# A recurrent attention with a token mixer: freely placed PSUM banks, work moved between engines, and a new order

## The chip, the cores and the metric

The kernel runs on one core of a Trainium2 chip. Its engines work side by side, each through its own list of instructions in order: TensorE (PE; its weight loads are a row of their own, PEld), VectorE (DVE), ScalarE (ACT), GpSimd (POOL), and SyncE (SP), which here only issues the transfers. TensorE writes into PSUM, a small memory of eight banks of 512 float32 columns on 128 partitions. The other memory is SBUF.

The metric is the time of the kernel on the device in microseconds, as a median over runs. "us" is microseconds.

## The reference

Two stages. The first is a linear attention with a state that decays (`B=4` batches, `H=8` heads, `S=768` tokens, `D=48`):

```python
for t in range(S):
    kt, vt, rt, wt = k[:, :, t], v[:, :, t], r[:, :, t], w[:, :, t]
    cur = einsum('bhd,bhe->bhde', u[None] * kt, vt)
    y[:, :, t] = einsum('bhd,bhde->bhe', rt, state + cur)
    state = wt[:, :, :, None] * state + einsum('bhd,bhe->bhde', kt, vt)
```

The second takes `x`, which is `y` with the heads side by side (4 x 768 x 384), and mixes the tokens of each batch:

```python
wq = x @ w_q                                   # 384 -> 64
wk = x @ w_k                                   # 384 -> 64
W_tok = 1/sqrt(64) * einsum('bsd,btd->bst', wq, wk)
mixed = einsum('bst,btd->bsd', W_tok, x)       # all tokens of the batch
out = maximum(mixed, 0.0) @ w_out              # 384 -> 384
```

All inputs and the output are float32. As no function stands between `W_tok` and `x`, the kernel computes `T = wk^T x` (64 x 384) for a batch and then `wq T`.

## The kernel before

The kernel works on 12 units, three for each batch. A unit is 256 tokens, that is two chunks of 128. Within a chunk the loop over tokens becomes matrix products. With `L` the running sum of the logarithms of `w`, `RT = r exp(L)` and `KT = k exp(-L)`, the products of tokens of one chunk are `A = KT^T RT`, masked to the past (`AM`), and the earlier chunks enter through a state `SB`. The operations of a unit, in the names that the profile uses:

| name | engine | what |
|---|---|---|
| wg, kg, rg, vg | SP queue | loads of w, k, r, v (384 KB each, v in four parts) |
| lw | ACT | logarithm of w, to bf16 |
| k, r (k16, r16), VB | POOL | casts to bf16 |
| cw | PE | running sums of lw |
| ep, en | ACT | exp(L), exp(-L), both from cw |
| kT, rT / ks | PE / DVE | transposes / copy of kT to SBUF |
| RT, qT | DVE | rT x ep, rT x ks |
| KT | DVE | ks x en, both in SBUF |
| dps, dd, Vd | PE, DVE, POOL | the term with u |
| A, AM | PE, DVE | products within a chunk, and the mask |
| kb, KD | PE, ACT | KT transposed back, scaled |
| sn, SB | PE, DVE | new state; scaled with ptm (POOL) |
| y, X | PE, ACT | output of the attention, scaled, to bf16 |
| xt, XT, qk, QK | PE, DVE, PE, ACT | X transposed; wq and wk of the unit |

After the third unit of a batch comes its mixer: T (PE), TS (ACT), mx (PE), MX (ACT, the maximum with 0), fp (PE, product with `w_out`), os (ACT), and the store.

The program's order is made by a small planner. Each step is added with an engine, an assumed duration, a rank, and the kind of buffer that it fills. The planner then plays the steps through on these assumptions: whenever an engine is free, the ready step of lowest rank for which a buffer is free starts. The instructions are emitted in the order of these starts, and each engine runs its own in that order.

```python
    NS = 2
    LATE = 60
    kinds = {"w": 3, "s": 2, "os": 3, "SB": 3}
    ...
    def wtile(dtype, name):      # two banks, three of them
        return ps.tile([C, 1024 if dtype == F32 else 2048], dtype, name=name, tag="w", bufs=3)

    def stile(dtype, name):      # one bank, two of them
        return ps.tile([C, 512 if dtype == F32 else 1024], dtype, name=name, tag="s", bufs=2)
    ...
        R = 100 * n              # n is the unit
        ...
        k16_ = add("POOL", 830, R + 10, f_c16(k16, kg), fill="k16", read=[lk_])
        r16_ = add("POOL", 830, R + 11, f_c16(r16, rg), fill="r16", read=[lr_])
        ...
        cw = add("PE", 500, R + 11, f_cw, fill="w", read=[ln])
        ...
        rT = add("PE", 460, R + 13, f_rawT("rT", r16), [kT], fill="s", read=[r16_])
        ...
        def f_KT():
            nc.vector.tensor_tensor(sb("KT", [C, 1024]), t["ks"], t["en"], ALU.mult)
        KT = add("DVE", 690, R + 14, f_KT, fill="KT", read=[ks, eno])
        ...
        for g in range(2):       # A by pairs of heads; each holds both chunks
            ...
            a = add("PE", 280, R + 20 + g, f_A, fill="w", read=[RT, KT])
            am.append(add("DVE", 1220, R + 20 + g, f_am, fill=f"AM{g}", read=[a]))
        ...
        x_ = add("ACT", 900, R + 30, f_x, read=[y0, y_])
        xt = add("PE", 360, R + 31, f_xt, [x_], fill="s")
        xts = add("DVE", 560, R + 32, f_xts, fill="XT", read=[xt])
        qk = add("PE", 680, R + 33, f_qk, [state["wts"]], fill="s", read=[xts])
        batch["qks"].append(add("ACT", 480, R + 34, f_qks, read=[qk]))
        if not last:
            return
        R += LATE
        T_ = add("PE", 1000, R + 35, f_T, batch["qks"] + batch["xs"], fill="s")
        Ts = add("ACT", 480, R + 36, f_Ts, read=[T_])
        for dt in range(NK):     # mx by thirds of the 384 channels, all tokens
            mx = add("PE", 200, R + 37 + dt, f_mx, [Ts], fill="w")
            rel.append(add("ACT", 880, R + 37 + dt, f_rl, read=[mx]))
        for ii in range(NU):     # fp by token blocks: each needs all of rel
            fp = add("PE", 1000, R + 41 + ii, f_fp, rel + [state["wts"]], fill="w")
            os_ = add("ACT", 880, R + 41 + ii, f_os, fill="os", read=[fp])
            add("SP", 1000, R + 42 + ii, f_st, read=[os_], lag=2000)
```

The bodies of most steps are cut here. In `f_T`, six matmuls (one for each chunk of the batch) sum into one bank.

Of the kernel before, what the change touches and what calls it, by code (L numbers as in the profile page):

```python
# [25 lines left out]
class Plan:  # L26
# [8 lines left out]
    def add(self, eng, dur, rank, fn, after=(), fill=None, read=(), lag=100):  # L35
        s = dict(eng=eng, dur=dur, rank=rank, fn=fn, after=[a for a in after if a is not None],
                 fill=fill, lag=lag, n=len(self.steps), out=[], reads=[])
        s["buf"] = None if fill is None else dict(kind=fill, left=0)
        for a in read:
            s["after"].append(a)  # L40
            if a["buf"] is not None:
                a["buf"]["left"] += 1
                s["reads"].append(a["buf"])
        self.steps.append(s)
        return s

    def order(self):
# [6 lines left out]
        free = dict(self.kinds)  # L54
        ready = [s for s in self.steps if not left[s["n"]]]
        running, done, eng_free, now = [], [], {}, 0
        while ready or running:
            ready.sort(key=lambda s: (s["rank"], s["n"]))
            started = True
            while started:  # L60
                started = False
                for s in ready:
                    if ready_at[s["n"]] > now or eng_free.get(s["eng"], 0) > now:
                        continue
                    if s["fill"] is not None:
                        if not free[s["fill"]]:
                            continue
                        free[s["fill"]] -= 1
# [13 lines left out]
            while running and running[0][0] <= now:  # L82
                t, n = heapq.heappop(running)
                s = self.steps[n]
                for buf in s["reads"]:
                    buf["left"] -= 1
                    if not buf["left"]:
                        free[buf["kind"]] += 1
# [10 lines left out]
def kernel(  # L99
# [48 lines left out]
    OS = [const([C, 2 * DM], F32, f"os{i}") for i in range(3)]  # L148
# [77 lines left out]
    LATE = 60  # L226
    kinds = {"w": 3, "s": 2, "os": 3, "SB": 3}
# [4 lines left out]
    for name in ("en", "ks", "qT", "RT", "KT", "ptm", "VB", "dd", "Vd", "AM0", "AM1", "KD", "XT"):  # L232
        kinds[name] = NS
    plan = Plan(kinds)

    def wtile(dtype, name):
        return ps.tile([C, 1024 if dtype == F32 else 2048], dtype, name=name, tag="w", bufs=3)

    def stile(dtype, name):
        return ps.tile([C, 512 if dtype == F32 else 1024], dtype, name=name, tag="s", bufs=2)  # L240

    def unit(n, state, batch):
# [4 lines left out]
        last = i == NU - 1  # L247
        t = {}
        R = 100 * n
        add = plan.add  # L250

        def sb(name, shape, dtype=BF16):
            t[name] = sm.tile(shape, dtype, name=name, tag=name, bufs=NS)
            return t[name]

        lw_ = add("SP", 1440, R, lambda: load(b, i, wg, w), fill="wg", lag=2000)
        lk_ = add("SP", 1440, R, lambda: load(b, i, kg, k), fill="kg", lag=2000)
        lr_ = add("SP", 1440, R, lambda: load(b, i, rg, r), fill="rg", lag=2000)

# [3 lines left out]
        lv = add("SP", 2200, R, f_lv, fill="vg", lag=2000)  # L263
# [5 lines left out]
        ln = add("ACT", 845, R + 10, f_ln, fill="lw", read=[lw_])  # L269
# [6 lines left out]
        k16_ = add("POOL", 830, R + 10, f_c16(k16, kg), fill="k16", read=[lk_])  # L276
        r16_ = add("POOL", 830, R + 11, f_c16(r16, rg), fill="r16", read=[lr_])

        def f_cw():
            t["cw"] = cw = wtile(F32, "cw")  # L280
# [7 lines left out]
        cw = add("PE", 500, R + 11, f_cw, fill="w", read=[ln])  # L288

        def f_ep():  # L290
            nc.scalar.activation(view(ep, 66, [[EW, 8], [-65, 2], [1, 64]]),  # L291
                                 t["cw"], ACT.Exp, bias=0.0, scale=1.0)
        epo = add("ACT", 1040, R + 12, f_ep, fill="ep", read=[cw])

        def f_en():
            nc.scalar.activation(sb("en", [C, 1024]), t["cw"], ACT.Exp, bias=0.0, scale=-1.0)  # L296
        eno = add("ACT", 1040, R + 12, f_en, fill="en", read=[cw])
# [9 lines left out]
        kT = add("PE", 460, R + 12, f_rawT("kT", k16), fill="s", read=[k16_])  # L307
        rT = add("PE", 460, R + 13, f_rawT("rT", r16), [kT], fill="s", read=[r16_])
# [3 lines left out]
        ks = add("DVE", 690, R + 13, f_ks, fill="ks", read=[kT])  # L312
# [3 lines left out]
        qT = add("DVE", 690, R + 13, f_qT, fill="qT", read=[rT, ks])  # L316

        def f_RT():
            nc.vector.tensor_tensor(
                view(sb("RT", [C, 1024]), 0, [[C, 8], [64, 2], [1, 64]]),  # L320
                view(t["rT"], 0, [[C, 8], [64, 2], [1, 64]]),
                view(ep, 0, [[EW, 8], [66, 2], [1, 64]]), ALU.mult)
        RT = add("DVE", 690, R + 15, f_RT, fill="RT", read=[rT, epo])

        def f_KT():
            nc.vector.tensor_tensor(sb("KT", [C, 1024]), t["ks"], t["en"], ALU.mult)  # L326
        KT = add("DVE", 690, R + 14, f_KT, fill="KT", read=[ks, eno])

        def f_ptm():
            nc.gpsimd.tensor_tensor(  # L330
                view(sb("ptm", [C, 16], F32), 0, [[2, 8], [1, 2]]),
                view(ep, 64, [[EW, 8], [0, 2]]),
                view(MB, 0, [[0, 8], [1, 2]]), ALU.mult)
        ptm = add("POOL", 220, R + 17, f_ptm, fill="ptm", read=[epo])
# [3 lines left out]
        vb = add("POOL", 830, R + 18, f_vb, fill="VB", read=[lv])  # L338
# [7 lines left out]
        dps = add("PE", 320, R + 18, f_dps, [state["ub"]], fill="s", read=[qT])  # L346
# [3 lines left out]
        dd = add("DVE", 170, R + 18, f_dd, fill="dd", read=[dps])  # L350

        def f_vd():
            nc.gpsimd.tensor_tensor(sb("Vd", [C, 2 * DM]), t["VB"],  # L353
                                    view(t["dd"], 0, [[1, 2 * H], [0, D]]), ALU.mult)
        vd = add("POOL", 1480, R + 19, f_vd, fill="Vd", read=[vb, dd])

        am = []
        for g in range(2):
            def f_A(g=g):
                t[f"A{g}"] = x = wtile(F32, f"A{g}")  # L360
                for hl in range(2):
                    for c in range(2):
                        hp = 2 * g + hl
                        col = (c * NP + hp) * C
                        for hh in range(2):
                            mm(x[:, ds(hh * 512 + (hl * 2 + c) * C, C)],
                               t["KT"][ds(hh * 64, D), ds(col, C)],
                               t["RT"][ds(hh * 64, D), ds(col, C)])
            a = add("PE", 280, R + 20 + g, f_A, fill="w", read=[RT, KT])

            def f_am(g=g):
                nc.vector.tensor_tensor(  # L372
                    view(sb(f"AM{g}", [C, 1024]), 0, [[C, 8], [1, C]]),
                    view(t[f"A{g}"], 0, [[C, 8], [1, C]]),
                    view(US, 0, [[0, 8], [1, C]]), ALU.mult)
            am.append(add("DVE", 1220, R + 20 + g, f_am, fill=f"AM{g}", read=[a]))

        nkb = 1 if last else 2

        def f_kb():  # L380
            t["kb"] = x = stile(BF16, "kb")
            for cp in range(NP * nkb):
                mm(x[:, ds(cp * C, C)], t["KT"][:, ds(cp * C, C)], ID16, trans=True)
        kb = add("PE", 240 * nkb, R + 21, f_kb, fill="s", read=[KT])

        def f_kd():
            nc.scalar.activation(sb("KD", [C, 1024])[:, ds(0, 512 * nkb)],  # L387
# [209 lines left out]
```

## Time and profile before

The kernel takes 134.17 us (median of three runs, 133.45 to 136.71). The profile is of an execution of 136.19 us, 134.5 us from the first instruction to the last.

| engine | operation | count | mean ns of one |
|---|---|---|---|
| DVE | AM, 1024 columns from PSUM | 24 | 1215 |
| DVE | KT, 1024 columns, both inputs in SBUF | 12 | 859 |
| DVE | ks, 1024 columns bf16 from PSUM | 12 | 688 |
| DVE | XT, 768 columns bf16 from PSUM | 12 | 555 |
| DVE | SB, 384 columns | 20 | 553 |
| POOL | Vd, 768 columns, both inputs in SBUF | 12 | 1478 |
| POOL | casts of k, r, v, 768 columns | 36 | 895, 872, 826 |
| ACT | ep, en, 1024 columns | 24 | 1047, 1023 |
| ACT | KD, 1024 columns (512 in four of them) | 12 | 1115 (684) |
| ACT | X, 768 columns | 12 | 900 |
| ACT | MX and os, 768 columns | 24 | 810, 805 |
| ACT | QK and TS, 384 columns | 16 | 475, 482 |
| PE | fp, 384 columns a matmul | 72 | 375 |

In such a row the shape is partitions by columns; an engine's time depends on the columns. The matmul's mean is its latency; matmuls in a row start closer together than that. A page of the profile also gives, for each engine, what ended its idle time ("A <- B" is: A stood idle until B was done), the granted clock of TensorE in tenths (PEclk, 9 is full), and the busy share of the 16 DMA engines. A timeline row gives the start, the length, the engine, the line, the operation with its output and inputs, and in brackets the idle time before it with what ended it.

### The profile page before, as it was taken

How to read it: one execution, taken by the hardware profiler on the slowest of the kernel's cores; microseconds unless marked ns; L12 is line 12 of the kernel's file. 1: busy time of each engine (PE TensorE's matmuls, PEld its weight loads, DVE VectorE, ACT ScalarE, POOL GpSimd, SP SyncE). 2: the span in 40 equal slices, each digit the busy share in tenths (PEclk: the TensorE clock that was granted, in tenths of full speed). 3: DMA queues.
4: the chain of work that ended last, by engine and by line, in shares of the span. 5: the costliest groups of instructions: out<-in, count | busy, mean ns of one | idle time of the engine just before them, and what ended most of it. 6: DMA issues, size and time to landing. Idle time of an engine off the chain costs nothing. (4 is left out here: it accounts for less than half of the span.)

```text
span 134.5 us, 3607 instructions
## 1 busy us (share of the span) xinstructions
PE 103.1 (77%) x1480; PEld 74.7 (56%) x1480; DVE 83.0 (62%) x132; ACT 80.8 (60%) x104; POOL 56.0 (42%) x79
## 2 busy tenths in 40 slices
PE   0378877787889996976898995497899976577940
PEld 0266655666656785855565784386666755432410
DVE  6457878889766588947629798219953798310000
ACT  3445565945789898358679792554789532226330
POOL 7345775647383661833852807236511404000000
PEclk9999999999999999599599999658999999975577
DMA  3999999989999999799999489699100650000084
GB/s 78 304 238 279 193 320 225 280 168 256 220 255 239 238 325 235 171 287 235 252 256 246 107 247 279 156 239 252 25 0 5 165 186 5 0 0 0 9 224 118
DMA packets 67871, 24.60 MB, mean 183 GB/s; under 512 B 64400, under 2 KB 67856, under 8 KB 67856
## 3 DMA queue, kind: packets, MB, share of 16 engines
q1 hardware_dynamic: 67440, 24.39, 73.2%
q8 instruction: 11, 0.18, 0.5%
q10 hardware_dynamic: 416, 0.00, 0.2%
q14 instruction: 4, 0.03, 0.1%
HBM read 19.66 MB, written 4.72 MB: 181 GB/s over the span
## 5 line engine op out<-in xcount | busy, mean ns | idle before, releaser
L372 DVE TENSOR_TENSOR AM<-A,US 128x1024 bf16<-128x1024 f32 x24 | 28.5, 1215 | 0.8 <-PE A L130 0.7
L353 POOL TENSOR_TENSOR Vd<-VB,dd 128x768 bf16<-128x768 bf16 x12 | 17.7, 1478 | 20.0 <-DVE dd L349 20.0
L442 ACT ACTIVATE X<-y,gx 128x768 bf16<-128x768 f32 x12 | 10.8, 900 | 10.3 <-PE y L130 10.3
L130 PE MATMUL cw<-CM,lw 64*128 64x128 bf16 x192 | 9.1, 247 | 10.0 <-ACT lw L266 10.0
L411 DVE TENSOR_TENSOR SB<-sn,ptm 128x384 bf16<-128x384 f32 x20 | 11.1, 553 | 8.7 <-PE sn L130 8.5
L130 PE MATMUL fp<-wo,MX 128*128 128x384 bf16 x72 | 15.7, 375 | 0.7 <-ACT MX L509 0.7
L266 ACT ACTIVATE lw<-wg 128x768 bf16<-128x768 f32 x12 | 10.1, 841 | 9.6 <-DMA wg<-in_w_dram 9.6
L291 ACT ACTIVATE ep<-cw 128x1024 bf16<-128x1024 f32 x12 | 12.6, 1047 | 5.5 <-PE cw L130 3.0
L337 POOL CAST VB<-vg 128x768 bf16<-128x768 f32 x12 | 9.9, 826 | 13.6 <-PE y L130 5.6
L387 ACT ACTIVATE KD<-kb,gv 128x1024 bf16<-128x1024 bf16 (+1 forms) x12 | 11.7, 971 | 5.1 <-PE kb L130 5.1
L273 POOL CAST k<-kg 128x768 bf16<-128x768 f32 x12 | 10.7, 895 | 8.7 <-DMA kg<-in_k_dram 8.6
L273 POOL CAST r<-rg 128x768 bf16<-128x768 f32 x12 | 10.5, 872 | 6.9 <-DMA rg<-in_r_dram 6.9
L311 DVE COPY ks<-kT 128x1024 bf16<-128x1024 bf16 x12 | 8.3, 688 | 8.1 <-PE kT L130 8.0
L130 PEld LDWEIGHTS <-lw 64*128 64x128 bf16 x192 | 6.7, 108 | 11.4 <-ACT lw L266 10.6
L456 DVE COPY XT<-xt 128x768 bf16<-128x768 bf16 x12 | 6.7, 555 | 10.0 <-PE xt L130 10.0
L130 PEld LDWEIGHTS <-KT 48*128 48x128 bf16 (+1 forms) x272 | 11.0, 99 | 2.5 <-DVE KT L326 0.7
L296 ACT ACTIVATE en<-cw 128x1024 bf16<-128x1024 f32 x12 | 12.3, 1023 | 0.0
L526 ACT COPY os<-fp 128x768 f32<-128x768 f32 x12 | 9.3, 805 | 4.4 <-PE fp L130 2.8
L130 PEld LDWEIGHTS <-MX 128*128 128x128 bf16 x72 | 7.5, 108 | 7.9 <-ACT MX L509 2.6
L476 ACT CAST QK<-qk 128x384 bf16<-128x384 f32 x12 | 5.7, 475 | 9.9 <-PE qk L130 9.9
L130 PEld LDWEIGHTS <-AM 128*128 128x128 bf16 x192 | 9.3, 102 | 3.5 <-DVE AM L372 1.3
L326 DVE TENSOR_TENSOR KT<-ks,en 128x1024 bf16<-128x1024 bf16 x12 | 10.3, 859 | 0.8
(61 smaller groups left out, 194.6 us busy)
## 6 DMA issues: line engine op xcount, KB each, us to landing
wg<-in_w_dram SPq DMA_DIRECT2D x12, 384.0 KB, 4.1
kg<-in_k_dram SPq DMA_DIRECT2D x12, 384.0 KB, 4.7
rg<-in_r_dram SPq DMA_DIRECT2D x12, 384.0 KB, 5.8
vg<-in_v_dram SPq DMA_DIRECT2D x48, 96.0 KB, 4.1
out_dram<-os SPq DMA_DIRECT2D x24, 192.0 KB, 3.0
wof<-in_moe_w_out_dram SPq DMA_DIRECT2D x1, 576.0 KB, 5.0
wqf<-in_moe_w_q_dram SPq DMA_DIRECT2D x1, 96.0 KB, 2.9
wkf<-in_moe_w_k_dram SPq DMA_DIRECT2D x1, 96.0 KB, 2.4
```

Of the source, the lines that this page charges most:

```text
L130: nc.tensor.matmul(o, l, rr, start=start, stop=stop, skip_group_check=True, is_transpose=trans)
L266: nc.scalar.activation(view(lw, 0, [[64, H], [512, 2], [1, D]]), view(wg, 0, [[D2, H], [D, 2], [1, D]]), ACT.Ln, bias=0.0, scale=math.exp( ...
L273: nc.gpsimd.tensor_copy(view(dst, 0, [[64, H], [512, 2], [1, D]]), view(src, 0, [[D2, H], [D, 2], [1, D]]))
L291: nc.scalar.activation(view(ep, 66, [[EW, 8], [-65, 2], [1, 64]]), t["cw"], ACT.Exp, bias=0.0, scale=1.0)
L296: nc.scalar.activation(sb("en", [C, 1024]), t["cw"], ACT.Exp, bias=0.0, scale=-1.0)
L326: nc.vector.tensor_tensor(sb("KT", [C, 1024]), t["ks"], t["en"], ALU.mult)
L337: nc.gpsimd.tensor_copy(sb("VB", [C, 2 * DM]), vg)
L353: nc.gpsimd.tensor_tensor(sb("Vd", [C, 2 * DM]), t["VB"], view(t["dd"], 0, [[1, 2 * H], [0, D]]), ALU.mult)
L372: nc.vector.tensor_tensor(view(sb(f"AM{g}", [C, 1024]), 0, [[C, 8], [1, C]]), view(t[f"A{g}"], 0, [[C, 8], [1, C]]), view(US, 0, [[0, 8], ...
L387: nc.scalar.activation(sb("KD", [C, 1024])[:, ds(0, 512 * nkb)], t["kb"][:, ds(0, 512 * nkb)], ACT.Copy, bias=0.0, scale=gv)
L411: nc.vector.tensor_tensor(view(x, 0, [[D, H], [1, D]]), view(t[f"sn{c}"], 0, [[D, H], [1, D]]), view(t["ptm"], c * 8, [[1, 8], [0, D]]), A ...
L442: nc.scalar.activation(view(X["t"], 2 * i * DM, [[DM, 2], [1, DM]]), view(t["y"], 0, [[512, 2], [1, DM]]), ACT.Copy, bias=0.0, scale=gx)
```

## The change

It has five parts.

1. PSUM becomes one tile of eight banks. The planner places each tile in any free bank, or in any two neighbouring free banks, instead of three fixed pairs and two fixed single banks. This is for tiles that waited for a slot of their kind.
2. KT, the key times its decay, goes from VectorE to GpSimd in all units but one. KD, XT, X, QK, MX and os get an engine for each unit from a table of letters. This is for evening out the engines.
3. The order comes from a table of ranks (`OFF`), one for each operation, found by a search over the planner's model. The planner also assumes other durations, and counts 260 ns after a TensorE step and 80 ns after others.
4. In the first and the last unit, en, ep, RT, KT, ptm, Vd, kb and KD are computed by chunks (512 columns at a time). In all units A and AM are now divided by chunk, and not by heads, so that y of chunk 0 needs only the first.
5. In all mixers mx is divided by token blocks and no longer by channels, so that each fp needs one MX only. In the last mixer X, XT, QK, TS, MX, fp, os and the store are halved, one half on ScalarE and the other on VectorE, and T takes its first four matmuls early.

```diff
+        banks = [True] * 8
+        def place(kind):
+            if kind == "w":
+                pairs = [x for x in range(7) if banks[x] and banks[x + 1]]
+                ...
+            ones = [x for x in range(8) if banks[x]]
+            ...
-    OS = [const([C, 2 * DM], F32, f"os{i}") for i in range(3)]
+    NOS = 4
+    OS = [const([C, 2 * DM], F32, f"os{i}") for i in range(NOS)]
...
-    LATE = 60
-    kinds = {"w": 3, "s": 2, "os": 3, "SB": 3}
+    STEP = 100
+    OFF = dict(load=-4, ln=207, c16=-50, cw=60, ex=34, rT=123, ks=-72, qT=284, RT=139, KT=27,
+               ptm=275, vb=34, dps=61, vd=-63, A=8, am=115, kb=94, kd=-148, sn=-109, sb=184,
+               y=108, x=-84, xt=129, xts=-98, qk=64, qks=249, T=148, mx=-51, rl=317, fp=103,
+               os=13, st=149)
+    ENG = dict(KT="PPPPPPPPPPDP", kd="DDADADDADDAD", xts="AAAAAAAAAAAD", x="AAADAAAAAAAA",
+               qks="DAAAAAAAAADA", rl="AAAADAAAAAAA", os="AADDDAADADAD")
+    SPLIT = (0, B * NU - 1)
+    kinds = {"os": NOS, "SB": 3}
...
+    kinds["MX"] = 4
+    PS = ps.tile([C, 4096], F32, name="PS", tag="PS")
-    def wtile(dtype, name):
-        return ps.tile([C, 1024 if dtype == F32 else 2048], dtype, name=name, tag="w", bufs=3)
+    def wtile(name):
+        return PS[:, ds(now["step"]["buf"]["bank"][0] * 512, 1024)]
...
+        end = n == B * NU - 1
+        fine = each if n in SPLIT else both
+            if lag is None:
+                lag = 260 if eng == "PE" else 80
+            step = plan.add(NAMES.get(eng, eng), dur, STEP * n + OFF[at] + more, fn, after, ...)
...
+            def f_KT(cs=cs, kte=kte):
+                e = nc.vector if kte == "D" else nc.gpsimd
+                e.tensor_tensor(sb("KT", [C, 1024])[:, cols(cs, 512)], t["ks"][:, cols(cs, 512)],
+                                t["en"][:, cols(cs, 512)], ALU.mult)
...
+        for c in range(2):
+            def f_A(c=c):          # one chunk, all heads
...
+        for p, cs in enumerate(each if end else both):
+            xe = "AD"[p] if end else ENG["x"][n]      # X; and so for XT, QK
...
+        groups = [[0, 1, 2, 3], [4], [5]] if end else [list(range(NCH))]     # T
...
         for ii in range(NU):
+            def f_mx(ii=ii):       # one token block, all channels
...
+            halves = each if end else both            # MX, fp, os, store
+                e = "AD"[p] if end else ENG["rl"][m]
```

## The prediction

> **What bounds the kernel now.** I read the page from the top, then the waits of TensorE, then three timelines (ScalarE, the SyncE queue, the end). First the busy rows and, below them, clock and DMA in 40 slices of 3.36 us.
>
> ```profile
> PE 103.1 (77%) x1480; PEld 74.7 (56%) x1480; DVE 83.0 (62%) x132; ACT 80.8 (60%) x104; POOL 56.0 (42%) x79
> ...
> PEclk9999999999999999599599999658999999975577
> DMA  3999999989999999799999489699100650000084
> ```
>
> No engine is full, the DMA engines are nearly full until slice 29 (about 97 us), then idle. So there is a load stage and, after it, 37 us in which the kernel only computes. Is the load stage bound by loads or by compute? The kernel has 12 units (256 tokens of one batch each). I take two marks per unit: the issue of its `w` load and its copy X<-y.
>
> ```profile
> 0.78 0.44 SPq L165 DMA_DIRECT2D wg<-in_w_dram  x1
> ...
> 42.35 0.58 SPq L165 DMA_DIRECT2D wg<-in_w_dram  x1
> ...
> 86.83 0.62 SPq L165 DMA_DIRECT2D wg<-in_w_dram  x1
> ```
>
> ```profile
> 17.15 0.90 ACT L442 ACTIVATE X<-y,gx 128x768 bf16<-128x768 f32 x1 [1.44 <-PE y L130]
> ...
> 72.06 0.90 ACT L442 ACTIVATE X<-y,gx 128x768 bf16<-128x768 f32 x1
> ...
> 116.04 0.90 ACT L442 ACTIVATE X<-y,gx 128x768 bf16<-128x768 f32 x1 [2.09 <-PE y L130]
> ```
>
> These are units 0, 6 and 11. From load to X unit 0 takes 16.4 us, unit 6 takes 29.7, unit 11 takes 29.2. Compute falls behind the loads, by 13 us. Its pace is (116.04 - 17.15)/11 = 8.99 us a unit. The bound is therefore the compute pipeline; loads come early and then wait for their buffers.
>
> What does a unit need of TensorE? Start-to-start distances at full clock in its timeline (20 to 45 us): cw .56, kT and rT .45 each, A .56, dps .27, kb .46, sn 2x.34, y 2x.53, xt .42, qk .65: 5.56 us. A batch adds T .97, mx 1.0, fp 18x.17 = 3.06: 5.0, or 1.68 a unit. Together 7.24 us. The pace of 8.99 is thus 1.75 us above what TensorE alone could do. Where that goes shows in TensorE's waits (total, times, longest):
>
> ```profile
> PE xt L130 <- DVE RT L319: 3.3, 4, 1.0
> ...
> PE xt L130 <- ACT KD L387: 0.8, 1, 0.8
> ...
> PE qk L130 <- DVE dd L349: 0.5, 1, 0.5
> PE dps L130 <- DVE RT L319: 0.5, 1, 0.5
> ```
>
> xt reads X, not RT. RT is the last reader of rT, and rT sits in one of the two single banks: xt waits for a bank. Such rows (these, and dps<-SB .4, sn<-dd .3, kT<-QK .2) come to 6.0 us. The rest is waiting on data in a fixed order, and half clock: PEclk drops to 5 and 6 where TensorE had gaps; in 82 to 92 us the granted clock is 0.66 and eight kT transposes start .85 us before the next group instead of .45.
>
> The end, after the last X:
>
> ```profile
> 118.99 0.48 ACT L476 CAST QK<-qk 128x384 bf16<-128x384 f32 x1 [2.05 <-PE qk L130]
> ...
> 121.74 2.22 ACT L509 ACTIVATE MX<-mx 128x768 bf16<-128x768 f32 x3 [0.60 <-PE mx L130]
> ...
> 124.01 5.30 PE L130 MATMUL fp<-wo,MX 128*128 128x384 bf16 x16 [0.20 <-ACT MX L509]
> ...
> 129.39 0.80 ACT L526 COPY os<-fp 128x768 f32<-128x768 f32 x1 [1.12 <-PE fp L130]
> ```
>
> This is one serial chain on TensorE and ScalarE with VectorE and GpSimd idle. fp needs all three MX parts (they are parts of its contraction), and runs at .32 us a matmul instead of .17 because the granted clock is 0.50 in 120 to 127 us.
>
> **What the Trainium skill says.** "SBUF — State Buffer", section "Who interferes with whom": a VectorE instruction with two SBUF inputs contends with a GpSimd instruction that reads SBUF, and the one that comes second is held. KT is the only such VectorE operation here, and the trace agrees: KT has a median of .693 us, but 1.41 us at 73.89 beside a GpSimd cast, which itself took 1.29 instead of .82. "GPSIMD Engine Reference", section "4.1 Engine selection": two-input elementwise work is about 2x slower on GpSimd. The trace can be compared through Vd: 1.478 us for 768 columns. "TensorE: Matmul & The Clock Gate", section "What's actually happening": activity releases the throttle, and idle windows of about 3.4 us bring half clock back. The trace shows half clock, though after shorter gaps (2.81 us before cw at 85.83). "PSUM — Partial Sum Buffer", section "PSUM bank collisions raise a hardware error ⚠️": two engines must not touch one bank in the same 32-partition group at once. So halves on ScalarE and VectorE run side by side only where they lie in other banks or other partitions; no run here shows a collision.
>
> **The change part by part.**
> (1) PSUM. Before: three slots of two banks and two of one. After: eight banks, a tile takes any free one or pair, so up to eight single tiles live at once. At most it removes the 6.0 us of bank waits, and it lets the order be freer. No instruction is added.
> (2) KT to GpSimd in 11 of 12 units. By columns, 1.478 x 1024/768 = 1.97 us each: GpSimd 56.0 + 11 x 1.97 = 77.7 us, 6.5 a unit, below TensorE's 7.24. VectorE loses 10.3 us and the port contention. A unit's chain gets 1.97 - .69 = 1.3 us longer; with double buffers that is latency, not pace.
> (3) Evacuations moved. ScalarE to VectorE: eight KD (five of 1.115, three of .684: -7.6 us on ScalarE; on VectorE, at the .69 that ks takes for the same shape and .42 for half, +4.7), one and a half X, two QK and the last one's halves, four full and three half output copies, one and three halves of MX, half the last TS (about 9 us less on ScalarE, 11 more on VectorE by the slope of 1.03 ns a column between SB and AM). XT goes the other way: -6.4 on VectorE, +9.3 on ScalarE at MX's .81. Sums: ScalarE 80.8 - 7.6 - 9 + 9.3 = 73.5, VectorE 83.0 - 9.6 (eleven of the twelve KT) - 6.4 + 4.7 + 11 = about 83. So engines are evened out, not relieved: all of ScalarE, VectorE, GpSimd lie at 73 to 83 us, TensorE at 12 x 7.24 = 87.
> (4) The order. Ranks per operation replace the hand-set ones (the plan also counts 260 ns after a matmul and 80 after others, instead of 100). This is where the gain of (1) to (3) is made or lost. Of the 1.75 us above TensorE's need I credit rather less than half, 0.8 us a unit: 11 x 0.8 = 8.8 us. That makes the pace 8.2 us.
> (5) First unit by chunks. Now the cast of r (7.68) stands behind ptm (7.52), which waits for ep; and A waits for whole RT and KT. With r first and half tiles of ep, en, RT, KT I take 1.0 us off.
> (6) The end. X in halves on two engines saves .4; xt and XT by halves .4; qk and QK .5; T with four of its six matmuls already done .5; MX by token block (fp's first block then needs only half-tile copies of about .45 us instead of 2.27 us of MX) 1.8, less .5 because fp then has 18 matmuls ahead of it instead of 16; the last os as two halves .35; a smaller last store .3; A by chunk, so that chunk 0 is done while the second mask runs, .4. Sum about 4.1; I keep 4.0. fp itself stays at half clock (18 x .32 = 5.8 us), since the tail still has gaps.
>
> Sum: 134.2 - 8.8 - 1.0 - 4.0 = 120.4 us.
>
> **The rivals.** (a) The loads become the bound. At a DMA share of 1 the stage moves about 246 GB/s (264/1.08, 240/.99 and 250/.99 in the windows 4.4 to 20, 20 to 35 and 35 to 50 us), and 19.66 MB read plus two batches of output, 2.36 MB, take 89.5 us. Twelve units can then not be loaded before about 91 us. From the w load of unit 11 at about 82 us, 16.4 us to X and 14.5 to the end give 113. That is a floor under my figure and speaks for a low end of about 113. (b) GpSimd in the chain. KT now queues behind casts that wait for DMA (8.6 and 6.9 us of such waits now) and in front of Vd; a KT that is late holds A, kb and everything after. For it: in-order queue, 2 us an instruction. Against it: GpSimd now idles 20.0 us in front of Vd. If it holds, the pace stays near 8.8 and only the end is gained: 128. (c) The order fits a model and not the chip, new head-of-line waits take the place of bank waits, or banks released in the plan are really released later: 133 to 138. (d) TensorE, denser, keeps its full clock in the middle, and the pace comes to 7.7: 115.
>
> **Range and chances.** (a) and (d) give 113 to 115, (b) 128, so 113.5 to 128.5 should hold it 8 times in 10. Faster by over 2% means under 131.5; only (c) misses it: 0.87. Within 2%: 0.07. Slower: 0.06.
>
> **What would show it.** X copies 8.2 us apart and the last one near 106; about 14.5 us from there to the end; no PE wait on a non-operand above 1 us in sum; GpSimd near 78 us busy, KT at 1.97; VectorE near 83; no 5 or 6 in PEclk in the middle; load-to-X lag of the last units near 20 us. I am wrong if X copies still stand 9 us apart, if GpSimd's KT is what A waits for, or if X follows the loads directly, with DMA full to the last load: then loads bind.

## The result, and the profile after

The changed kernel takes 125.94 us (median of four runs, 125.04 to 128.82), the kernel before, run beside it, 134.84 (133.45 to 136.71). The ratio is 0.939, with an interval of 0.927 to 0.951. The gain is 8.9 us; 13.8 were predicted.

The page of the changed kernel, its busy row and the rows of clock and DMA, in 40 slices of 3.08 us:

```profile
PE 96.1 (78%) x1528; PEld 71.7 (58%) x1528; DVE 84.6 (69%) x139; ACT 75.6 (61%) x105; POOL 77.4 (63%) x96
...
PEclk9999999999999999967999999999999999995875
DMA  3999989996999979999979688989899760000663
```

The engines stand where the prediction put them: GpSimd rose from 56.0 to 77.4, ScalarE fell to 75.6, VectorE stayed. All of PSUM is now one tile, PS, and all matmuls have one line, L161, so that groups are told apart by the other operand.

The X copies of units 0, 6 and 11 (the last as two halves; this is the later one, on VectorE), from the timeline of the changed kernel:

```profile
16.80 0.90 ACT L299 ACTIVATE X<-PS,gx 128x768 bf16<-128x768 f32 x1 [0.85 <-ACT ep L406]
...
67.98 0.89 ACT L299 ACTIVATE X<-PS,gx 128x768 bf16<-128x768 f32 x1
...
106.25 0.62 DVE L303 TENSOR_SCALAR X<-PS,gx 128x384 bf16<-128x384 f32 x1 [0.49 <-PE PS L161]
```

The pace is (106.25 - 16.80)/11 = 8.13 us a unit; it was 8.99. The SyncE queue, in the same view:

```profile
6.40 0.62 SPq L197 DMA_DIRECT2D wg<-in_w_dram  x1
...
43.20 4.42 SPq L718 DMA_DIRECT2D out_dram<-os  x6
47.66 0.61 SPq L197 DMA_DIRECT2D wg<-in_w_dram  x1
...
69.87 3.99 SPq L718 DMA_DIRECT2D out_dram<-os  x6
73.90 0.61 SPq L197 DMA_DIRECT2D wg<-in_w_dram  x1
...
88.11 0.62 SPq L197 DMA_DIRECT2D wg<-in_w_dram  x1
```

The loads of `w` for units 6 and 9 (47.66 and 73.90) stand directly behind the six stores of a batch. Those stores wait for the output copies, and the queue is in order. The load pace, (88.11 - 6.40)/10 = 8.17, is the pace of the X copies. From load to X the last unit now takes 18 us instead of 29.

What TensorE waits for (total, times, longest):

```profile
PE PS L161 <- ACT lw L374: 7.3, 3, 5.3
PE PS L161 <- ACT X L299: 3.6, 6, 0.8
PE PS L161 <- POOL KT L447: 2.2, 6, 1.2
```

5.3 us of the first row is the wait for the first load. Of the rows that named a tile which was no operand ("xt <- RT", 6.0 us before) 1.3 us are left: the transpose of the first r waits .8 us for ks, and mx .5 us for ep. The end, from the timeline:

```profile
109.43 0.47 ACT L297 CAST TS<-PS 64x384 bf16<-64x384 f32 x1
109.94 0.56 DVE L301 CAST TS<-PS 64x384 bf16<-64x384 f32 x1 [0.93 <-ACT TS L297]
...
111.42 4.78 PE L161 MATMUL PS<-wo,MX 128*128 128x384 bf16 x18 [0.20 <-ACT MX L307]
...
112.97 7.56 SPq L718 DMA_DIRECT2D out_dram<-os  x12
...
116.24 0.56 DVE L301 COPY os<-PS 128x384 f32<-128x384 f32 x1 [0.42 <-PE PS L161]
```

The last output copy is done at 116.80, the last store is issued at 120.53, and the end is at 123.3. The two spans, 134.5 and 123.3, differ by 11.2 us. Of these 9.4 lie between the first X and the last, .35 before and 1.4 after. (The profiled execution of before, 136.19 us, was one of the longer ones and had a mean granted clock of .905; that of after, 125.04, the shortest, .952. So the 11.2 us flatter the change; the medians differ by 8.9.)

### The profile page after: what moved, and what is told of

Its sections match the earlier page's. It is cut to its first block, busy times and chain, and to the rows that moved or that the text cites. A ratio compares the mean times of both kernels' runs of the same rounds, so it can differ in the third digit from the quotient of the medians.

```text
span 123.3 us, 3766 instructions
## 1 busy us (share of the span) xinstructions
PE 96.1 (78%) x1528; PEld 71.7 (58%) x1528; DVE 84.6 (69%) x139; ACT 75.6 (61%) x105; POOL 77.4 (63%) x96
## 4 chain that ended last, share of the span: by engine, by line
PE 33%; SPq 18%; ACT 14%; DMA 12%; POOL 9%; issue 6%; DVE 3%; ACTq 0%; POOLq 0%
PE PS L161 33%; POOL KT L447 8%; DMA wg<-in_w_dram 8%; SPq L197 7%; SPq L204 7%; ACT ep L406 5%; ACT en L400 5%; DMA vg<-in_v_dram 3%; SPq L718 2%; ACT lw L374 1%; ACT XT L297 1%; DVE os L301 1%; POOL ptm L453 1%; ACT QK L297 1%; SPq L727 1%
## 5 line engine op out<-in xcount | busy, mean ns | idle before, releaser
L496 DVE TENSOR_TENSOR AM<-PS,US 128x1024 bf16<-128x1024 f32 x24 | 28.8, 1218 | 3.4 <-PE PS L161 3.3
L447 POOL TENSOR_TENSOR KT<-ks,en 128x1024 bf16<-128x1024 bf16 (+1 forms) x13 | 23.7, 1824 | 4.6 <-DVE ks L425 2.4
L478 POOL TENSOR_TENSOR Vd<-VB,dd 128x768 bf16<-128x768 bf16 (+1 forms) x14 | 18.0, 1291 | 4.9 <-DVE dd L473 4.5
L400 ACT ACTIVATE en<-PS 128x1024 bf16<-128x1024 f32 (+1 forms) x14 | 12.6, 902 | 9.3 <-PE PS L161 7.2
L161 PE MATMUL PS<-CM,lw 64*128 64x128 bf16 x192 | 8.7, 240 | 7.5 <-ACT lw L374 7.3
L161 PE MATMUL PS<-wo,MX 128*128 128x384 bf16 x72 | 14.0, 356 | 0.2 <-ACT MX L307 0.2
L161 PEld LDWEIGHTS <-KT 48*128 48x128 bf16 (+1 forms) x272 | 10.6, 98 | 6.2 <-POOL KT L447 3.3
L297 ACT COPY XT<-PS 128x768 bf16<-128x768 bf16 (+1 forms) x12 | 9.2, 768 | 6.7 <-PE PS L161 6.7
L542 DVE TENSOR_TENSOR SB<-PS,ptm 128x384 bf16<-128x384 f32 x20 | 11.1, 553 | 2.7 <-PE PS L161 2.5
L406 ACT ACTIVATE ep<-PS 128x1024 bf16<-128x1024 f32 (+1 forms) x14 | 12.9, 919 | 0.0
L299 ACT ACTIVATE X<-PS,gx 128x768 bf16<-128x768 f32 (+1 forms) x11 | 9.6, 870 | 4.0 <-PE PS L161 3.1
L161 PEld LDWEIGHTS <-lw 64*128 64x128 bf16 x192 | 6.5, 105 | 8.7 <-ACT lw L374 7.7
L161 PEld LDWEIGHTS <-MX 128*128 128x128 bf16 x72 | 7.3, 105 | 5.7 <-issue 1.6
L161 PE MATMUL PS<-RT,KT 48*128 48x128 bf16 x192 | 8.8, 225 | 1.6 <-POOL KT L447 1.0
L161 PEld LDWEIGHTS <-AM 128*128 128x128 bf16 x192 | 8.7, 99 | 2.0 <-issue 0.3
```

Of the source, the lines that this page charges most:

```text
L161: nc.tensor.matmul(o, l, rr, start=start, stop=stop, skip_group_check=True, is_transpose=trans)
L297: nc.scalar.copy(o, i)
L299: nc.scalar.activation(o, i, ACT.Copy, bias=0.0, scale=by)
L400: nc.scalar.activation(sb("en", [C, 1024])[:, cols(cs, 512)], t["cw"][:, cols(cs, 512)], ACT.Exp, bias=0.0, scale=-1.0)
L406: nc.scalar.activation(view(ep, cs[0] * NP * EW + 66, [[EW, NP * len(cs)], [-65, 2], [1, 64]]), t["cw"][:, cols(cs, 512)], ACT.Exp, bias=0 ...
L447: e.tensor_tensor(sb("KT", [C, 1024])[:, cols(cs, 512)], t["ks"][:, cols(cs, 512)], t["en"][:, cols(cs, 512)], ALU.mult)
```

## The experiments

Executions of one kernel spread by up to 5 us with the granted clock, and in some rows most of them, in others none, had a low one: the lowest runs compare like with like, the medians only in part. Each difference is to the kernel before on the same chip; rows with the same "before" ran on the same chip. The lowest run of the kernel before was 133.45 to 134.61 us in four groups of runs, so a difference of about 1 us between two chips says nothing.

| run | median | lowest | before: median, lowest | difference of medians, of lowest |
|---|---|---|---|---|
| whole last stores | 128.48 | 124.90 | 137.65, 134.61 | -9.2, -9.7 |
| late stores | 122.05 | 121.93 | same | -15.6, -12.7 |
| both | 121.03 | 120.79 | same | -16.6, -13.8 |
| v loads left out | 125.52 | 124.74 | same | -12.1, -9.9 |
| changed kernel again | 127.69 | 124.82 | 137.44, 134.61 | -9.8, -9.8 |
| KT on VectorE | 129.75 | 129.53 | same | -7.7, -5.1 |
| fixed banks | 138.86 | 136.03 | same | +1.4, +1.4 |
| ranks set by hand | 128.62 | 126.76 | same | -8.8, -7.9 |
| no chunks, no halves | 133.04 | 132.00 | 136.54, 134.09 | -3.5, -2.1 |
| both, and the tail's edits | 120.72 | 119.91 | same | -15.8, -14.2 |
| BEFORE with late stores | 130.96 | 128.79 | same | -5.6, -5.3 |
| ranks by hand, fixed banks | 135.02 | 132.30 | same | -1.5, -1.8 |

My theory after the result: in the stage of the units the stores in the load queue set the pace of the changed kernel (a consequence of the faster compute), and the issue of twelve small stores sets its end. Rivals: the bandwidth of the loads sets the pace; or compute does, and then the question is which part of the change made it faster.

**Whole last stores.** The last batch's six half outputs are stored as three whole ones, in 6 transfers of 192 KB instead of 12 of 96 KB.

```diff
-                    add("SP", 560 * len(cs), "st", f_st, more=6 * ii, cs=cs, ...)
+                    if p == len(halves) - 1:      # both chunks at once
+                        add("SP", 1120, "st", f_st, more=6 * ii, use=[go], lag=2000)
```

> The last mixer's six half outputs (96 KB a transfer, twelve transfers) go out as three whole ones (six transfers of 192 KB), each after both of its halves. Theory: the end of the changed kernel is the issue of the twelve transfers on the SyncE queue, 7.56 us from 112.97 us on, so that the last leaves 3.7 us after the last os copy has ended. With six, the last leaves about 1.3 us after it: 2.3 us faster than the changed kernel, about 0.98 of it, 123.6 us. Rival: the end is the landing of the bytes, which are the same: no change, or 0.3 us slower because each store waits for its second half.

Alone it shows no gain: its lowest run has the time of the changed kernel's lowest. In its profile the last store is issued 2.57 us after the last output copy (123.37 and 120.80) instead of 3.73, but then 3.5 us pass until the end instead of 2.8.

**Late stores.** The stores of the first three batches are issued after the last load (nine output tiles instead of four). The order of all other engines is the same.

```diff
-    OS = [const([C, 2 * DM], F32, f"os{i}") for i in range(NOS)]
+    OS = [const([C, 2 * DM], F32, f"os{i}") for i in range(9)]
+            if s["fn"].__name__ == "f_st" and loads < B * NU:
+                held.append(s)        # issued after the last load
+                continue
```

> The stores of the first three batches are issued after the load of the last unit; the order of all other engines is kept. Theory that loads now bind: the stores of batch 0 and 1 hold the queue for 4.4 and 4.0 us (and wait about 2 us for os), so the loads of unit 6 and of unit 9 come that much earlier, the w load of unit 11 goes from 88 us to about 80, and the X copies from 8.13 to about 7.6 us apart: 4 to 6 us faster than the changed kernel, 120 to 122 us. Rival, that compute on TensorE in its fixed order sets the pace and loads only look late: w loads come earlier, X copies stay 8.1 us apart, under 1 us faster.

It gains 2.9 us by the lowest runs (-12.7 against -9.8) and 5.9 by the medians (-15.6 against -9.8). Its clock row and TensorE's first waits:

```profile
PEclk9999999999999999999999999999999999996785
```

```profile
PE PS L161 <- ACT lw L374: 5.4, 1, 5.4
PE PS L161 <- ACT X L299: 3.6, 6, 0.8
```

Only the start's wait for `lw` is left, the clock is full up to the end, and `w` of unit 11 is issued at 79.46 instead of 88.11. The X copies are (103.41 - 17.36)/11 = 7.82 apart. The spread is gone too: four runs lie within .3 us.

**Both.**

> Both of the two edits, late stores and whole last stores. If the two causes are separate, the gains add: 6 to 8 us faster than the changed kernel, 118 to 120 us. If loads do not bind, it is that of the whole stores alone, about 123.6 us. If the nine held stores now stand in front of the last ones in the queue, part of the gain at the end is lost.

1.0 us less than late stores alone, on the same chip. Of the .9 us between the two profiles (119.9 and 119.0) .6 lie ahead of the first X (17.36 and 16.74), which the edit doesn't touch, and .5 behind the last one (16.5 and 16.0).

**v loads left out from unit 3 on.** The kernel leaves out 36 of the 48 transfers of v, and later units compute with the v of the first three. It separates the bandwidth of the loads from their place in the queue.

```diff
+            if n < NB:
                 load_v(b, i, vg, 0)
                 load_v(b, i, vg, 1)
```

> The loads of v are left out from unit 3 on (later units use the v of the first three), which takes 36 of 48 v transfers and 24 of 24 to 25 thousand packets of 192 B down to a quarter; all compute is kept. Theory that loads bind: the pace of X falls from 8.13 to about 7.4, TensorE's need of 7.24 plus little: 6 to 9 us faster, 117 to 120 us. Rival, that compute binds: under 1.5 us faster.

The bandwidth theory falls: 3.5 MB less are loaded, and against before the lowest run gains what the changed kernel's gains (-9.9 and -9.8); by the medians it is 2.3 us more, where the late stores, with every load in place, have 5.9. The DMA row of its page, and what the SyncE queue waited for (in this kernel the store is L719):

```profile
DMA  2999999899990068999900899899000850000662
```

```profile
SPq L719 <- ACT os L297: 35.0, 3, 14.4
SPq L719 <- DVE os L301: 7.6, 1, 7.6
```

DMA stands empty in slices 13, 14, 21 and 22, because the queue stands at a store and waits for its output copy. `w` of unit 6 is issued at 47.27, as in the changed kernel (47.66), though nothing was in its way but the stores. So the bandwidth does not set the pace of this kernel. Whether it would with the stores out of the way was not tried.

**The changed kernel again**, for comparison on one chip with the next three.

> The changed kernel once more, unaltered, so that the next three can be compared with it on the same chip. All theories: 124 to 129 us.

**KT on VectorE.**

```diff
-                e = nc.vector if kte == "D" else nc.gpsimd
+                e = nc.vector
```

> KT on VectorE in all twelve units, everything else as after the change. If moving KT is needed to even out the engines: VectorE goes from 84.6 to about 92 us busy (11 x .69), GpSimd from 77.4 to 54, and the time rises by 2 to 6 us because VectorE is held by KT just where A, sn and qT need it. If KT on GpSimd is only latency in a stage that the loads' queue sets: the same within 1.5 us.

2.1 us (medians) to 4.7 us (lowest) come back; the ratio to before is 0.958 (0.948 to 0.967). VectorE's busy time rises to 92.9 us, and TensorE's wait for qT from 1.6 and 2.3 us (two profiles of the changed kernel) to 4.5 us: KT stands in VectorE's list ahead of what TensorE needs next. So in this order the move pays, although an instruction takes three times as long on GpSimd. The edit does not tell the planner: it still counts KT as GpSimd's work. What KT on VectorE would cost in an order made for it was not tried.

**Fixed banks.** PSUM's places limited to pairs at banks 0, 2, 4 and single tiles in 6 and 7; the planner makes its order anew.

```diff
-                pairs = [x for x in range(7) if banks[x] and banks[x + 1]]
+                pairs = [x for x in (0, 2, 4) if banks[x] and banks[x + 1]]
-            ones = [x for x in range(8) if banks[x]]
+            ones = [x for x in (6, 7) if banks[x]]
```

> PSUM again as three fixed pairs and two fixed single banks, order of the planner made anew for it. If free banks are a main part of the gain, 5 us or more come back as waits of TensorE for tiles that are not its operands (they were 6.0 us before the change): 131 us or more. If the ranks and the places of work carry the gain and the queue of loads sets the pace, less than 2.5 us come back.

11.2 us come back, more than the whole gain. TensorE's lines in its timeline show how:

```profile
91.15 0.49 PE L161 MATMUL PS<-ID,X 128*128 128x128 bf16 x6 [0.85 <-DVE ks L425]
...
104.53 0.61 PE L161 MATMUL PS<-ID,k 128*128 128x128 bf16 x8
109.56 0.50 PE L161 MATMUL PS<-ID,X 128*128 128x128 bf16 x6 [0.24 <-ACT QK L297]
...
111.73 0.62 PE L161 MATMUL PS<-ID,r 128*128 128x128 bf16 x8
```

The transpose of X waits for ks, the copy of kT, which it doesn't read: it waits for a single bank. Such waits come to about 2.8 us (an estimate: the sum of those in its timeline that end with a tile which the waiting group does not read). Two larger losses stand in the trace. One is in the order: the planner puts the transpose of the last unit's r 7.2 us behind that of its k (111.73 and 104.53), since xt and qk of two units pass through the two single banks first. In the changed kernel the two stand 2.1 us apart (97.40 and 99.46). All of the last unit's work then hangs on it, ScalarE is idle 5.88 us ahead of the last X, and from the X of unit 10 to the last it takes 4.7 us more (9.44 and 4.74). The other comes before: the X of unit 10 is already 6.7 us later than in the changed kernel (108.17 and 101.51). Here a load stands behind stores:

```profile
75.25 4.46 SPq L718 DMA_DIRECT2D out_dram<-os  x6
79.75 0.60 SPq L197 DMA_DIRECT2D wg<-in_w_dram  x1
...
85.16 1.03 PE L161 MATMUL PS<-CM,lw 64*128 64x128 bf16 x16 [2.77 <-ACT lw L374]
```

TensorE waits 2.77 us, and then the clock is .50 from 84 to 90 us. In the changed kernel the wait behind the same stores is 1.21 us (ahead of 79.94), at the full clock from 80 to 84. So the 11.2 us are not the banks alone; what part the stores have in them is not separated.

**Ranks set by hand**, those of the kernel before in place of the searched ones; banks, places, chunks and halves as after.

```diff
-    OFF = dict(load=-4, ln=207, c16=-50, cw=60, ex=34, rT=123, ...)
+    OFF = dict(load=0, ln=10, c16=10, cw=11, ex=12, rT=12, ...)
```

> The ranks set by hand as before the change, with free banks, the engines' letters, the chunks and the halves of after. If the search for the order carries the gain (my term of 8.8 us): 132 us or more, X copies 9 us apart. If banks and the evening out of the engines carry it: within 3 us of the changed kernel.

Only .9 (medians) to 1.9 us (lowest) come back; the ratio to before is 0.938 (0.924 to 0.952), the same as that of the changed kernel (0.939). With free banks, the search is not where most of the gain is.

**No chunks, no halves.**

```diff
-    SPLIT = (0, B * NU - 1)
+    SPLIT = ()
-        end = n == B * NU - 1
+        end = False
```

> No work by chunks in the first and last unit and no halved last mixer, everything else as after the change. By the terms of my prediction (1.0 at the start, 4.0 at the end) 5 us come back: about 131. By the two traces (first X .35 us earlier, last X to the end 1.4 us shorter) 2 us or less come back: 126 to 128.

Against before 6.2 us (medians) to 7.7 us (lowest) come back, as much as my two terms or more, but not where they were. Its last two X copies:

```profile
104.94 0.89 ACT L299 ACTIVATE X<-PS,gx 128x768 bf16<-128x768 f32 x1
112.38 0.90 ACT L299 ACTIVATE X<-PS,gx 128x768 bf16<-128x768 f32 x1 [4.93 <-PE PS L161]
```

They are 7.4 us apart, in the changed kernel 4.7 (101.51 and 106.25). The spans differ by 7.0: .4 before the first X, 3.1 from there to that of unit 10, 2.7 between these two, .9 after the last. The chunks of the last unit shorten its chain ahead of X. The 3.1 us in the middle come with an order made anew; what they are stays open.

**Both, and the tail's edits.** On top of "both": TS whole on ScalarE, both parts of a QK tile on one engine, and two of the last six stores issued from ScalarE's queue.

```diff
-                    copy("AD"[c], batch["TS"][ds(c * 64, 64), :], ...)     # two halves
+                    nc.scalar.copy(batch["TS"], batch["T"][:, ds(0, DM)])
-                copy("DA"[p], batch["QK"][ds(c0 * 64, 64), ...
+                copy("AD"[p], batch["QK"][ds(c0 * 64, 64), ...
+                        if end and j == 1 and ii > 0:      # after the last output copy
+                            other.append(issue)            # for nc.scalar
```

> The version with late and whole stores, and in the last mixer three edits: TS whole on ScalarE instead of 64 partitions on each of two engines, the two parts of QK that share a bank on one engine, and two of the last six stores issued from ScalarE's queue after its last copy. If the issue of the stores and the hand-over of one bank between two engines are what keeps the end long: TS .6 us less, last issue 1.5 us earlier after the last copy, together 119 us where the version without them has 121. If TensorE's fp and the landing of the last store set the end: 121 within .5.

Against before nothing measurable is gained over "both" (-15.8 and -14.2 against -16.6 and -13.8). Its timeline, and the DMA row of its page in slices of 2.95 us:

```profile
106.94 0.48 ACT L660 CAST TS<-PS 128x384 bf16<-128x384 f32 x1 [0.93 <-PE PS L161]
107.48 0.68 PE L161 MATMUL PS<-QK,TS 64*128 64x128 bf16 x18 [0.57 <-ACT TS L660]
...
110.69 3.24 SPq L718 DMA_DIRECT2D out_dram<-os  x4
...
111.19 1.58 ACTq L718 DMA_DIRECT2D out_dram<-os  x2
111.53 0.56 DVE L301 COPY os<-PS 128x384 f32<-128x384 f32 x1 [0.42 <-PE PS L161]
```

```profile
DMA  2999899899998998999999998959988888000095
```

TS to the last mx operand takes .54 us instead of 1.12 (109.43 to 110.55 in the changed kernel), as expected. From the last output copy (112.09) to the last issue (113.93) it is 1.84 us, with "both" 2.36. But then 4.1 us pass until the end at 118.0, and 3.2 with "both". The Trainium skill, "DMA: Bandwidth & Descriptors", section "Issuing engines are not separate DMA queues", says that a second issuing engine saves only issue time, since all run on the same 16 DMA engines; the run agrees: the landing took what the issue gave. The DMA row shows why: it ends with 9 and 5 tenths, that of the changed kernel with 6, 6 and 3. Here the DMA engines are .99 busy from 112 to 116 us; with twelve small stores they were .65 busy from 114 to 121 us. So in the changed kernel the issue sets the end, and with the issue made short the landing does. (From the last X to the end this profile has 14.3 us, that of "both" 16.0. Of the difference 1.6 is fp at the full clock, 3.10 against 4.73; whether the edits kept the clock up is not shown.)

**BEFORE with late stores.** The kernel before, with the hold of the stores alone.

```diff
-    OS = [const([C, 2 * DM], F32, f"os{i}") for i in range(3)]
+    OS = [const([C, 2 * DM], F32, f"os{i}") for i in range(9)]
+            if s["fn"].__name__ == "f_st" and loads < B * NU:
+                held.append(s)
+                continue
```

> The kernel BEFORE the change, with the stores of its first three batches issued after the last load (nine output tiles instead of three), the order of all other engines kept. If the stores in the load queue became the bound only through the change: no gain, 133 to 138 like before, with loads issued earlier but X copies still 9 us apart. If they cost 4 us in any kernel: 130 to 131 on a chip where before has 134.5.

My theory falls here, and with it a sentence of the prediction: the stores cost the kernel before 5.3 to 5.6 us as well. The X copies come 8.47 us apart instead of 8.99. Lines of its timeline, of the kernel before:

```profile
74.71 3.98 SPq L533 DMA_DIRECT2D out_dram<-os  x6
78.73 0.60 SPq L165 DMA_DIRECT2D wg<-in_w_dram  x1
...
84.93 0.84 ACT L266 ACTIVATE lw<-wg 128x768 bf16<-128x768 f32 x1 [3.18 <-DMA wg<-in_w_dram]
...
85.83 1.04 PE L130 MATMUL cw<-CM,lw 64*128 64x128 bf16 x16 [2.81 <-ACT lw L266]
```

and of the run with late stores, with its clock row:

```profile
78.17 0.57 SPq L165 DMA_DIRECT2D wg<-in_w_dram  x1
...
80.84 0.83 ACT L266 ACTIVATE lw<-wg 128x768 bf16<-128x768 f32 x1
```

```profile
PEclk9999999999999999999999999999999999959595
```

In the kernel before, `w` of unit 10 is issued behind the six stores, lw waits 3.18 us for it, and cw of unit 10 waits for lw. In TensorE's list this cw stands ahead of y of unit 8, so two units of work wait behind a load that "comes early". After the gap the clock is .50 from 86 to 90 us. With late stores (where 78.17 is the load of unit 11 and 80.84 the lw of unit 10) the wait and the half clock are gone, and the last X comes at 110.21 instead of 116.04.

**Ranks by hand and fixed banks.** Both edits of above.

> Ranks set by hand AND PSUM in fixed pairs and single banks; places of work, chunks and halves as after the change. If free banks carry the gain by themselves: about 136 us or more, against 128 with hand ranks and free banks. If the searched ranks only clash with fixed banks (the ranks were found for free ones): 130 us or less, as hand ranks were made for fixed banks.

With the places of work, the chunks, the halves and the new division of A and mx alone, the gain is 1.5 to 1.8 us. So free banks are worth some 6 to 7 us under the ranks set by hand (-8.8 and -7.9 against these), and the searched ranks, without free banks, are worse than those by hand (+1.4 against -1.5 and -1.8): they fit only the memory that they were found for.

## Why the prediction was right in its direction and too large

**What bounds it.** "The bound is therefore the compute pipeline; loads come early and then wait for their buffers" was wrong, for both kernels. I read it from the lag between a unit's load and its X. That lag contains the depth to which the plan works ahead; what counts is whether an engine that works in order stands still for a load at the head of its list. That wait was in my own text, as the 2.81 us before cw at 85.83, and I used it only to speak of the clock. Rival (a) had the right resource and the wrong reason: not the bandwidth (no v, no gain), but the stores' place in the queue. By the lowest runs it costs 5.3 us before and 2.9 after, by the medians 5.6 and 5.9. With late stores in both kernels the change is worth 7.4 us by the lowest runs (-12.7 and -5.3), with the stores in their place 9.8: up to 2.4 us of the gain may be a shorter wait for loads (TensorE's longest one for lw after the start fell from 2.81 to 1.21), and the runs don't settle how much.

**The sum.** My terms came from an execution of 136.19 us, and I took them from a median of 134.17. The two profiles differ by 11.15 us in time, so 13.8 were 2.65 too many: 2.6 too many at the end, .65 at the start, and .6 too few between the X copies. The other 2.25 us to the 8.9 of the medians are there because the profiled execution of before was a long one and that of after the shortest.

**(1) and (4), banks and order.** Predicted 8.8 us at 8.2 us a unit, with the banks as a ceiling of 6.0 inside it. The two profiles have 9.4 us at 8.13. In the medians about 7.1 would be left of it (an estimate: 8.9 - .35 - 1.4), so the size was about right and the nearness of 8.13 to 8.2 is in part luck. Two of my signs failed: PEclk has a 6 and a 7 in the middle, and the waits for tiles that are not operands are 1.3 us, not under 1. The credit was wrong: I put it under the order. The ladder of the runs is -1.5 to -1.8 (places, chunks, halves), 6 to 7 more with free banks, and 1 to 2 more with the searched ranks. It is one way up of several. Taken out of the whole change one at a time, KT's place costs 4.7 us by the lowest runs, free banks 11.2, chunks and halves 7.7 and the searched ranks 1.9: 25.5 us of a gain of 9.8. The parts need each other and can't be added, which my sum did. My ceiling was about the worth of the banks in the ladder. It came from TensorE's waits for tiles that it doesn't read, but with fixed banks such waits are only some 2.8 us: the rest came by the order (the r of the last unit, 7.2 us behind k) and by a wait for a load.

**(2) KT.** Predicted 1.97 us each and 77.7 us busy; measured 2.12 (median of the whole tiles) and 77.4. The Trainium skill, "GPSIMD Engine Reference", section "4.1 Engine selection", has about 2x for such work; here it is 2.12 against .68 for the one KT that stayed on VectorE, 3.1x, and the measurement decides. Rival (b) fell: TensorE waits 2.2 us for KT in all, and with KT back on VectorE in the same order the kernel is slower. I misread one line: the KT of 1.41 us at 73.89 stood beside Vd (73.27 to 74.75), which was not slowed; the cast that began at 74.69 was (1.29 instead of .82).

**(3)** held: 75.6 and 84.6 us busy, predicted 73.5 and 83. (Eleven KT of .859 are 9.4 us, not 9.6.)

**(5)** Predicted 1.0, measured .35 (first X 16.80, before 17.15). In other runs with the same first unit it comes at 16.70 to 17.36, so the .35 shows nothing.

**(6), the end, is the step that failed.** Predicted 4.0 from the last X to the end, measured 18.46 - 17.05 = 1.4. In pieces, from the two timelines:

| piece | before | after | gain | predicted |
|---|---|---|---|---|
| last X to TS | 4.62 | 3.18 | 1.44 | 1.8 |
| TS to first fp | 1.94 | 1.99 | -.05 | 1.3 with the next |
| fp to its end | 6.71 | 4.78 | 1.93 | |
| to the end of the last os | .88 | .60 | .28 | .35 |
| to the last store issued | 1.27 | 3.73 | -2.46 | .3 with the next |
| to the end | 3.04 | 2.77 | .27 | |

Down to the end of the last output copy 3.45 us were predicted and 3.60 measured, about 1 of them by luck: fp ran at a clock of .70 where I had .50 (4.78 us against 18 x .32 = 5.8). The mis-sized term is "a smaller last store .3": from the last copy to the end it is not .3 us less but 2.2 more (6.50 and 4.31). I looked at the bytes of a store and not at the issue of many. Halving the outputs doubled the transfers to 12, and at .63 us of issue each (7.56/12) the queue is busy from the first output copy on for 7.56 us, whatever fp does. A second profile of the changed kernel shows it:

```profile
113.70 3.10 PE L161 MATMUL PS<-wo,MX 128*128 128x384 bf16 x18 [0.20 <-ACT MX L307]
...
114.90 7.56 SPq L718 DMA_DIRECT2D out_dram<-os  x12
```

Here fp ran at full clock, 1.7 us shorter than in the first profile, and yet the end came 16.8 us after the last X (125.3 - 108.53), not 15.4. With whole stores it is 16.0 (119.0 - 102.98 in "both"), .5 us less than with halved ones (119.9 - 103.41 in "late stores"). So the halves are only a part of the 2.2 us: from the last copy to the end whole stores still take 5.5 us. The first of them is issued only at 111.86, 1.6 us before the last copy is done, as the second half of the first block is copied that late. And a part that I had not counted lies ahead of the last X: it comes 4.74 us after that of unit 10, before the change 6.48, without chunks and halves 7.44. These 1.7 us are inside the 9.4. (My term "A by chunk .4" belongs there too, and not to the end.)

**The range.** 125.94 lies in it, 2.6 us from its upper end, because the terms that were too large were small beside the pace. Rival (d), a clock that stays full in the middle and a pace of 7.7, is where the late stores lead: full clock, 7.82 to 7.86 a unit.

## What to carry to other kernels

Do not judge whether loads bind by how long before their use they are issued, but by whether an in-order engine waits for one at the head of its list; and look at what stands ahead of that load in its own queue, above all at stores, which wait for the end of a chain. Holding the stores back until the loads are out was worth 5.3 us in one kernel and 2.9 in the other (lowest runs) for a few more output tiles, and together with whole stores it gives 121.03 us, better than both kernels. Halving work over two engines pays where the chain runs through it, but it also doubled the transfers, and a queue that issues one in .63 us then set the end; half the transfers gave back .5 us, and with the issue shortened once more the DMA engines were full. Halves by partition (TS as 64 x 384) take as long as the whole. And parts of a change that were tuned together can't be priced one by one: here the four that were taken out cost 25.5 us of 9.8.

## What the runs showed that I had not expected

- TS, 64 partitions on each of two engines, took .47 on ScalarE and then .56 on VectorE, one after the other; the whole takes .48. The two halves are in one bank. The Trainium skill, "PSUM — Partial Sum Buffer", section "PSUM bank collisions raise a hardware error ⚠️", forbids two engines in one bank only within the same group of 32 partitions, and these are in different ones. Here the second half waited for the first by a semaphore all the same; why is open.
- The same 18 matmuls of fp in the same kernel took 4.78 us in one execution (clock .70 in 110 to 114 us) and 3.10 in another.
- In the changed kernel two gaps of TensorE of 1.2 and .9 us (ahead of 51.34 and 53.93, the second a wait for lw) stand before a mean clock of .60 from 53 to 56 us. A single gap of 1.2 us (ahead of 79.94) was followed by the full clock from 80 to 84 us. What decides is not shown.
- Late stores vary by .3 us over four runs, "both" by .4, the changed kernel by 4.4. The kernel before with late stores still varies by 4.7 us, so the stores alone are not the cause of the spread.
